# A new order of steps for a fused sigmoid-attention and token-mixing kernel

## The chip, the cores and the metric

The kernel runs on one core of one Trainium2 chip. The metric is the device time of one execution in microseconds (us). The engines named below are TensorE (PE), VectorE (DVE), ScalarE (ACT), GpSimd (POOL) and SyncE (SP), which issues most of the transfers between the chip's main memory and its on-chip memory (SBUF). TensorE writes its products to PSUM, a small memory of eight banks, from which DVE and ACT fetch ("evict") them.

## The reference

```python
# q, k, v: (8, 12, 448, 64) float32; w_q, w_k: (768, 64); w_out: (768, 768)
scores = q @ k^T / sqrt(64) - log(448)
attn   = 1 / (1 + exp(-scores)) @ v                      # per batch entry and head
x      = attn, heads side by side: (8, 448, 768)
wq, wk = x @ w_q, x @ w_k                                # (8, 448, 64)
W_tok  = wq @ wk^T / sqrt(64)                            # (8, 448, 448)
out    = relu(W_tok @ x) @ w_out                         # (8, 448, 768)
```

The kernel multiplies wk^T with x first (a 64 x 768 matrix, `tmp`) and then wq with that, so that the 448 x 448 matrix never exists.

## The kernel before

The work is cut into 24 quads: one batch entry u and four heads each, three quads to a batch entry. For every quad there are seven score steps (`scores`, letter S in the plan, 168 in all). A score step is four 64x64 matmuls (L319) into a pair of PSUM banks and one sigmoid on ACT over 128x896 (L324) into one of 16 buffers `at`. Seven value steps (`values`, letters P, p and R) multiply the sigmoids with v (L341). The last one evicts the sum to `xt`, either in one piece (L350) or in halves on DVE and ACT (L348).

Before its score steps a quad needs q and k as bf16 with the head dimension on the partitions. The letters of the plan choose the way for each quad:

- `a`, `b`: whole 128x128 transposes on PE (L237), one eviction for q and one for k (L293).
- `q`, `k`: 64x64 transposes on PE (L229), one eviction for both (L307).
- `c`, `d`: POOL exchanges blocks of 32-bit words between partition groups through a buffer named `swap`, in six copies of 32x448 words (`arrange`, L161, L164, L167); then DVE transposes q and k in blocks, with two instructions of 128x448 (L276).
- `r`, `s`, `z`: no exchange on POOL; DVE transposes whole (L269, two) and then in quarters (`quadrants`, L245, four of 32x448).

For `c` and `r` the casts to bf16 (L192) also reorder the data. v is cast at L209, the casts of `a` and `q` quads stand at L215. A cast goes to POOL unless the list of loads marks it with a dot or a capital, in which case a digit in the plan says when DVE (`1`) or ACT (`2`) does it.

For each batch entry the mixing part follows: `tr_x` (x and X) transposes `xt` back on PE (L379 small, L363 whole) with evictions at L392 and L368; `mlp_wqk` (W whole, L416; L tiled, L404, with an extra sum at L411 and L412) gives wq and wk; `mlp_wkn` (N) transposes wk (L431, evicted at L437); `mlp_tmp` (U, L445, or T, tiled, L460 with L464 and L465) and `mlp_mix` (M and G; L484, L498) follow, with the relu on DVE (L471) or ACT (L469). The output steps (O, Q, I) multiply with w_out: `out_pair` (L530) for the batch entries 2 to 5, `out_halves` (L570) and `out_chunk` (L611) for the others, evicted at L541, L543, L575, L576, L633 and L644, and stored.

Nothing is scheduled by a planner at build time. The string PLAN is the order: each letter issues one step, on whatever engines it uses, and every engine works in that order and waits where it must. The string BANKS names the PSUM banks of each step in turn. The string ORDER is the order of loads and casts; `pump_loads` issues a load as soon as the load eight places before it has been cast, and from the load number LATE on only two for each finished output. `pump` gives POOL its casts as soon as the buffers allow. An `F` is a filler matmul on zeros (L821). Before the plan starts, quad 0 is loaded, cast and transposed in parts (L676 to L803).

Of the kernel before, what the change touches and what calls it, by code (L numbers as in the profile page):

```python
# [17 lines left out]
def kernel(  # L18
# [12 lines left out]
    nc = tc.nc  # L31
# [4 lines left out]
    P = 128  # L36
# [11 lines left out]
    def pool(name, bufs, **kw):  # L48
# [16 lines left out]
    banks16 = banks.rearrange("p b x -> p (b x)").bitcast(BF16).rearrange("p (b x) -> p b x", b=8)  # L65

    BANKS = (
# [11 lines left out]
    )  # L79
    BANKS = BANKS.split()[::-1]  # L80

# [43 lines left out]
    def xt(u, j):  # L125
        return xts[u % 2 * NJ + j]


    TW = (1, 2,)


    PLAN = (
        "FFSSSFFKSSF11aSSbFFrSFSFSSFSqSPPsPPSPzkPSPSPPPSxSrSsPPPPSPPS"
        "PSPPPPSSXWzSSwWWSWWXSNSSPPPrSsPPUSPPzSPSPSPCMPPPSPSqkSSMSXSM"
        "SCcPPPSPPxSPdPSOSwwrSSwwWWxSOSSOsOSNPPSPPzCPSPPSIISISIcPSPdP"
        "PSPS2SPPOOSxSUSPPSMPPPcSPPSdOwWwSSMWWWoSMPPSPPPP1SSPcdOQSxSO"
        "OSSNCSOOXcdSSOOSTSPPPSrPPCPSPPCPPSPPPSPSOwowSSSwsOzOxSwwWPSP"
        "MSPPPPRSScSdXXOXoSMSOoNSMPPSPcPPSPPSUdSOSMOSOMoPSPPcPPSPSdPw"
        "WXWSMSWWWXSSONOScTSOSOSOOdSPOSrOSPPPGPPSPPPSPPsPSPOSPOSOzSQS"
        "XPcPPSPPPSPOSOdSOSxOlLlSLlLPSPPPxPP2GSPOOScOmdOSOOSNO1SQSTPP"  # L140
        "PcS1PPSPOPSOSOQSMOSOSOdScOOSdOMSOmOP2PSPPxSPPP12SOSOSOSxOllL"
        "SllcSLPPPSPPPSPOOdSxSOOSOSOSONQSTPSPPPSPPPSPPPxPPmPPLxLlMlGL"
        "lOOyOoNIItIiIMimIiMOoOOOoOoOOOOOOOOOoOO"
    )
    KIND = ["a"] + [t for t in PLAN if t in "qacer"]

    ld = {}
    SRC = dict(q=q, k=k, v=v)
# [3 lines left out]
    def arrange(n, eng):  # L152

        arranged.add(n)
        if KIND[n] in "er":
            return
        w = pq[n].rearrange("p e t i d y -> p e (t i d y)").bitcast(U32)
        z = p_one.tile([P, 2 * NI * 32], U32, tag="swap", name="swap")
        for g in range(2):
            lo, hi = slice(64 * g, 64 * g + 32), slice(64 * g + 32, 64 * g + 64)  # L160
            eng.tensor_copy(out=z[lo], in_=w[hi, 0])  # L161
        for g in range(2):
            lo, hi = slice(64 * g, 64 * g + 32), slice(64 * g + 32, 64 * g + 64)
            eng.tensor_copy(out=w[hi, 0], in_=w[lo, 1])  # L164
        for g in range(2):
            lo = slice(64 * g, 64 * g + 32)
            eng.tensor_copy(out=w[lo, 1], in_=z[lo])  # L167

    def load1(n, nm, eng):
        u, j = quads[n]  # L170
        if KIND[n] in "cer" and nm != "v":
            t = p_ld.tile([P, 2 * NI * HD], F32, tag="ld", name=nm + "32")
            eng.dma_start(
                out=t, in_=SRC[nm][u, 4 * j : 4 * j + 4].rearrange("h (p r) d -> (h p) (r d)", r=2 * NI),
            )
            ld[nm, n] = t
            return
        t = p_ld.tile([P, 2, NI * HD], F32, tag="ld", name=nm + "32")
        eng.dma_start(
            out=t,  # L180
            in_=SRC[nm][u, 4 * j : 4 * j + 4].rearrange(
                "(g h) (p i) d -> (h p) g (i d)", g=2, i=NI
            ),
        )
        ld[nm, n] = t

    def cast1(n, nm, e):
        if KIND[n] in "cer" and nm != "v":
            if n not in pq:
                pq[n] = p_c16.tile([P, 2, 2, NI, 32, 2], BF16, tag="qk16", name="qk16")  # L190
            f = pq[n]
            COPY[e](  # L192
                out=f[:, :, "qk".index(nm)].rearrange("p e i d y -> p e y i d"),
                in_=ld.pop((nm, n)).rearrange("p (y i e d) -> p e y i d", y=2, i=NI, e=2),
            )
            ld[nm + "16", n] = f
            if ("q16", n) in ld and ("k16", n) in ld:
                arrange(n, nc.gpsimd)
            return
        if nm == "v":  # L200
            t16 = p_v16.tile([P, 2, NI, HD], BF16, tag="v16", name="v16")
            if e == "d":
                u, j = quads[n]
                nc.gpsimd.dma_start(
                    out=t16.rearrange("p b i d -> p b (i d)"),
                    in_=v[u, 4 * j : 4 * j + 4].rearrange("(g h) (p i) d -> (h p) g (i d)", g=2, i=NI),
                )
            else:
                COPY[e](  # L209
                    out=t16.rearrange("p b i d -> p (b i d)"), in_=ld.pop((nm, n)).rearrange("p b x -> p (b x)"),  # L210
                )
            ld["v16", n] = t16
            return
        t16 = p_c16.tile([P, NI, 2, HD], BF16, tag=nm + "16", name=nm + "16")
        COPY[e](  # L215
            out=t16.rearrange("p i b d -> p b i d"),
            in_=ld.pop((nm, n)).rearrange("p b (i d) -> p b i d", i=NI),
        )
        ld[nm + "16", n] = t16
# [41 lines left out]
    def tr(n, nm, kind):  # L261
# [3 lines left out]
        if kind == "r":  # L265
# [2 lines left out]
            for e in range(2):  # L268
                nc.vector.transpose(out=qk[n][:, e].rearrange("p t i n -> p (t i n)").bitcast(F32), in_=w[:, e])  # L269
            return  # L270
        if kind in "cdef":
            assert n in arranged
            w = pq[n].rearrange("p e t i d y -> p e (t i d y)").bitcast(F32)[:, t]
            if t == 0:
# [417 lines left out]
    for t in wqks:  # L692
# [1 line left out]


    ORDER = (
# [4 lines left out]
    )  # L701
    BY = {"s": [], "v": []}
    for x in ORDER.split():
# [7 lines left out]
    done = dict.fromkeys("SPqkKxWNUMOCgz", 0)  # L711
    used, loaded, cast = set(), set(), set()

    LATE = 44
    ring = [("q", 0), ("k", 0)]

    allowed = [2]
# [94 lines left out]
    used |= {("q", 0), ("k", 0)}  # L812
    pump()

    ALIKE = dict(a="q", c="q", e="q", r="q", b="k", d="k", f="k", s="k", j="k", h="k", X="x", y="x", Y="x", g="g", z="z", L="W", l="W", T="U", t="U", I="O", i="O", Q="O", G="M", R="P")
    done["q"] = done["k"] = 1
    quads_r = []

    for t in PLAN:
# [18 lines left out]
        elif kind in "qk":  # L838
# [4 lines left out]
            tr(c, kind, t)  # L843
            if t in "df":
                used.add(("q", c))
            if t not in "cers":
                used.add((kind, c))
                pump()
        elif t == "g":
# [69 lines left out]
```

## Time and profile before

| | |
|---|---|
| median of 3 timed runs | 183.79 us (182.34 to 184.23) |
| the profiled execution, first to last instruction | 180.4 us; the page gives no other time for it |
| PE busy | 170.3 us (94%) |
| ACT busy | 159.0 us (88%) |
| DVE busy | 143.7 us (80%) |
| POOL busy | 122.9 us (68%) |
| granted TensorE clock | 1.000 |
| moved by DMA | 47.29 MB, mean 262 GB/s |

The page counts an engine as busy from the start of an instruction to its end; overlapping instructions are counted once, so a group's busy time can be below its count times its mean. Idle time of an engine is put down to what released it. A busy PE is not PE at its peak, since matmuls are pipelined and their ends are modelled.

### The profile page before, as it was taken

What the parts mean: (1) busy time and instruction counts of PE and PEld (TensorE: products, weight loads), DVE (VectorE), ACT (ScalarE), POOL (GpSimd) and SP (SyncE); (2) the same over time, 40 slices, a digit from 0 to 9 for tenths busy, and PEclk for the clock granted to TensorE, in tenths of its full rate; (3) what the DMA queues carried; (4) which work ended last, traced back from release to release, by engine and by line L of the source; (5) the groups of instructions that cost most, each with busy time, mean ns of one, the idle gap of its engine ahead of it and who ended that gap; (6) DMA issues with size and microseconds to landing.
All of it is one profiled execution on the core that took longest, in us unless ns stands there. A gap on an engine that the chain in (4) does not pass through costs nothing.

```text
span 180.4 us, 7849 instructions
## 1 busy us (share of the span) xinstructions
PE 170.3 (94%) x3412; PEld 114.1 (63%) x3412; DVE 143.7 (80%) x226; ACT 159.0 (88%) x208; POOL 122.9 (68%) x167
## 2 busy tenths in 40 slices
PE   7898899889999999999999999999999999999990
PEld 7444445444675555546667786677888888888660
DVE  3566899998988896989999999978789885868351
ACT  4599999999999999999999999998999989976310
POOL 1076899798999999999999999889978810010000
PEclk9999999999999999999999999999999999999999
DMA  5999999999999989699997999968596432505876
GB/s 169 353 394 346 325 385 376 283 304 366 339 305 358 349 266 299 226 318 349 279 318 277 257 307 329 372 215 272 137 336 166 131 88 48 137 4 123 207 196 174
DMA packets 24914, 47.29 MB, mean 262 GB/s; under 512 B 3888, under 2 KB 18480, under 8 KB 24880
## 3 DMA queue, kind: packets, MB, share of 16 engines
q1 hardware_dynamic: 23600, 44.64, 76.8%
q0 software_dynamic: 800, 1.18, 3.6%
q10 hardware_dynamic: 480, 0.98, 1.5%
q8 instruction: 26, 0.43, 0.9%
q14 instruction: 8, 0.07, 0.1%
HBM read 35.78 MB, written 11.01 MB: 259 GB/s over the span
## 4 chain that ended last, share of the span: by engine, by line
PE 61%; DMA 16%; ACT 7%; POOL 5%; DVE 4%; SPq 3%; issue 2%; POOLq 0%
PE banks L530 15%; PE banks L341 11%; PE banks L319 11%; PE banks L611 9%; DMA k<-in_k_dram 8%; ACT at L324 7%; DMA v<-in_v_dram 5%; DMA w<-in_moe_w_k_dram 4%; PE banks L570 3%; POOL qk L192 2%; PE banks L404 2%; PE banks L416 2%; PE banks L379 2%; PE banks L363 2%; PE banks L484 1%
## 5 line engine op out<-in xcount | busy, mean ns | idle before, releaser
L324 ACT ACTIVATE at<-banks 128x896 bf16<-128x896 f32 x168 | 139.8, 951 | 2.9 <-PE banks L319 2.4
L319 PE MATMUL banks<-qk 64*64 64x448 bf16 x672 | 62.0, 357 | 3.3 <-ACT at L324 2.0
L341 PE MATMUL banks<-at,v 64*64 64x448 bf16 x672 | 47.3, 351 | 0.8 <-ACT at L324 0.7
L319 PEld LDWEIGHTS <-qk 64*64 64x64 bf16 x672 | 25.7, 105 | 21.5 <-issue 13.3
L530 PE MATMUL banks<-wout,mx 64*64 64x384 bf16 x672 | 36.2, 323 | 0.0
L192 POOL CAST qk<-k 128x896 bf16<-128x896 f32 x19 | 22.7, 1196 | 10.1 <-DMA k<-in_k_dram 9.7
L341 PEld LDWEIGHTS <-v 64*64 64x64 bf16 x672 | 23.2, 106 | 8.4 <-issue 1.8
L350 DVE CAST xt<-banks 128x896 bf16<-128x896 f32 x22 | 23.8, 1084 | 2.5 <-PE banks L341 2.0
L530 PEld LDWEIGHTS <-mx 64*64 64x64 bf16 x672 | 22.6, 107 | 4.5 <-issue 0.2
L611 PE MATMUL banks<-wout,mx 128*128 128x384 bf16 (+1 forms) x138 | 24.4, 320 | 0.0
L192 POOL CAST qk<-q 128x896 bf16<-128x896 f32 x18 | 21.5, 1193 | 2.5 <-DVE qk L276 1.0
L471 DVE TENSOR_SCALAR mx<-banks 128x1024 bf16<-128x1024 f32 (+3 forms) x22 | 21.3, 970 | 1.9 <-PE banks L484 0.7
L209 POOL CAST v<-v 128x896 bf16<-128x896 f32 x22 | 20.6, 952 | 1.8 <-DMA v<-in_v_dram 1.3
L611 PEld LDWEIGHTS <-mx 128*128 128x128 bf16 x138 | 12.3, 98 | 9.8 <-issue 3.2
L167 POOL COPY qk<-swap 32x448 uint32<-32x448 uint32 x28 | 16.3, 584 | 1.6
L276 DVE STREAM_TRANSPOSE qk<-qk 128x448 f32<-128x448 f32 x28 | 17.0, 628 | 0.5 <-POOL qk L164 0.4
L161 POOL COPY swap<-qk 32x448 uint32<-32x448 uint32 x28 | 15.6, 556 | 2.5 <-DVE qk L192 0.8
L164 POOL COPY qk<-qk 32x448 uint32<-32x448 uint32 x28 | 15.6, 555 | 1.6
L245 DVE STREAM_TRANSPOSE qk<-qk 32x448 f32<-32x448 f32 x24 | 15.3, 636 | 0.6
L413 POOL COPY wq<-wqk 64x448 bf16<-64x448 bf16 x3 | 1.7, 556 | 15.8 <-DVE wqk L412 15.8
L644 DVE COPY o<-banks 128x384 f32<-128x384 f32 x12 | 6.6, 553 | 5.7 <-PE banks L611 5.3
L392 DVE COPY xn<-banks 128x1024 bf16<-128x1024 bf16 (+1 forms) x14 | 8.8, 625 | 2.8 <-PE banks L379 2.7
(89 smaller groups left out, 203.8 us busy)
## 6 DMA issues: line engine op xcount, KB each, us to landing
q<-in_q_dram SPq DMA_DIRECT2D x24, 448.0 KB, 6.3
v<-in_v_dram SPq DMA_DIRECT2D x24, 448.0 KB, 6.0
k<-in_k_dram SPq DMA_DIRECT2D x23, 448.0 KB, 6.9
out_dram<-o SPq DMA_DIRECT2D x50, 192.0 KB, 4.2
wout<-in_moe_w_out_dram POOLq DMA_DIRECT2D x2, 576.0 KB, 11.6
wout<-wout SPq DMA_DIRECT2D x12, 96.0 KB, 6.4
out_dram<-o ACTq DMA_DIRECT2D x4, 192.0 KB, 3.2
k<-in_k_dram SPq DMA_DIRECT2D x1, 256.0 KB, 4.8
```

Of the source, the lines that this page charges most:

```text
L161: eng.tensor_copy(out=z[lo], in_=w[hi, 0])
L167: eng.tensor_copy(out=w[lo, 1], in_=z[lo])
L192: COPY[e](out=f[:, :, "qk".index(nm)].rearrange("p e i d y -> p e y i d"), in_=ld.pop((nm, n)).rearrange("p (y i e d) -> p e y i d", y=2, ...
L209: COPY[e](out=t16.rearrange("p b i d -> p (b i d)"), in_=ld.pop((nm, n)).rearrange("p b x -> p (b x)"),)
L276: nc.vector.transpose(out=qk[n][:, t].rearrange("p t i n -> p (t i n)").bitcast(F32), in_=w)
L319: nc.tensor.matmul(sc[HALF[h], g, 0:S], qk[n][HALF[g], h, 1, i, :], qk[n][HALF[g], h, 0].rearrange("p i n -> p (i n)"), start=True, stop=True,
L324: inst = nc.scalar.activation(at, sc[:, :, 0:S], ACTF.Sigmoid, bias=attn_bias, scale=attn_scale)
L341: nc.tensor.matmul(ps[HALF[g], h, 0:S], ld["v16", n][HALF[h], g, i, :], ats[n, i][HALF[h], g, :], start=(i == 0), stop=(i == NI - 1),)
L350: read(fb, COPY[eng](out=xt(u, j)[:, :, 0:S], in_=ps[:, :, 0:S]))
L471: inst = nc.vector.tensor_scalar(dst, ps, moe_scale, 0.0, ALU.mult, ALU.max)
L530: nc.tensor.matmul(ps[HALF[x], y, 0:NB], mx[HALF[y], u, b, 64 * (i - 3 * y) : 64 * (i - 3 * y) + 64], wout16[HALF[y], slot(y, b), x * NB : ...
L611: nc.tensor.matmul(ps, mxs[w][:, 2 * S * c + m * P : 2 * S * c + (m + 1) * P], wout16[:, c, w0:w1], start=(c == 0), stop=(c == NC - 1),)
```

## The change

PLAN, BANKS and ORDER are replaced by new strings, and LATE falls from 44 to 30. The quads' ways change: before, one `a`, two `q`, six `r` and fourteen `c` follow quad 0; after, four `q`, sixteen `c` and three of a new kind `v`. For a `v` quad the six exchange copies of `arrange` are issued on DVE, just ahead of its two block transposes, in place of POOL. The way with transposes in quarters is no longer used.

Counted over the whole program, the order of the instructions shows further: 13 v casts on DVE instead of 1 (POOL 11 instead of 22, ACT none instead of 1); five `xt` evictions in halves instead of two; 21 small `tr_x` instead of 14 and 3 whole instead of 10; four tiled `mlp_wqk` instead of three; three tiled `mlp_tmp` instead of five; five filler matmuls instead of ten. The output steps keep their forms and numbers; 48 of the L530 matmuls that stood after the last score step stand before it.

```diff
-    KIND = ["a"] + [t for t in PLAN if t in "qacer"]
+    KIND = ["a"] + [t for t in PLAN if t in "qacerv"]
...
     def arrange(n, eng):
 
         arranged.add(n)
-        if KIND[n] in "er":
+        if KIND[n] in "r":
             return
...
-        if KIND[n] in "cer" and nm != "v":
+        if KIND[n] in "crv" and nm != "v":
...
             if ("q16", n) in ld and ("k16", n) in ld:
-                arrange(n, nc.gpsimd)
+                if KIND[n] == "v":
+                    arranged.add(n)
+                else:
+                    arrange(n, nc.gpsimd)
...
-        if kind in "cdef":
+        if kind == "v":
+            arrange(n, nc.vector)
+        if kind in "cdefv":
...
     ORDER = (
-        ".q1 .k1 k2 q2 q3 v0 w2 k3 v1 k4 q4 v2 w0 k5 q5 w1 v3 W5 v4 q6 k6 w4 k7 v5 q7 v6 q8 k8 k9 "
-        "q9 v7 q10 v8 k10 v9 k11 q11 k12 k13 v10 .q12 q13 v11 v12 v13 q14 k14 k15 q15 v14 q16 k16 "
-        "v15 q17 k17 k18 q18 q19 v16 v17 v18 k19 V19 W3 q20 .q22 q21 k20 W6 k21 .k22 v20 q23 k23 "
-        "v21 .v22 v23 "
+        "q1 .k1 v0 .k2 q3 .q2 v1 k3 q4 k4 w0 k5 .v2 q5 w1 v4 .v3 q6 k6 w4 k7 v5 q7 .k8 q8 k9 q9 "
+        "v6 v7 q10 v8 q11 k10 .k11 q12 k12 .v9 v11 .v10 k13 q13 .k14 .v12 v13 q14 q15 k15 v14 "
+        "q16 .k16 .v15 k17 q17 .v16 k18 .q19 q18 .v17 k19 k20 .v18 q20 .v19 q21 k21 k22 .v20 q22 "
+        ".v22 q23 k23 v21 .v23 "
     )
...
-    LATE = 44
+    LATE = 30
```

The beginning and the end of the plan, before and after:

```diff
-        "FFSSSFFKSSF11aSSbFFrSFSFSSFSqSPPsPPSPzkPSPSPPPSxSrSsPPPPSPPS"
+        "FFSSSFFKSSFSq1SkSRSP1Sp1SSpPqkRPSpSPSpSvppRPSSXdS1SqSkSRpPSS"
...
-        "SllcSLPPPSPPPSPOOdSxSOOSOSOSONQSTPSPPPSPPPSPPPxPPmPPLxLlMlGL"
-        "lOOyOoNIItIiIMimIiMOoOOOoOoOOOOOOOOOoOO"
+        "OQSoNcSQSOSQdoSOSOSRR1ppSppRSTQSQSo1SORPSPPPPpRpSpRGRMPRRmlll"
+        "ylllyIiyNIIIUiiGmiMQOQoOOOooOOoOoQoOOQQ"
```

More of the change, by code (lines that the diff above doesn't have):

```diff
@@ L126, in xt @@
         return xts[u % 2 * NJ + j]
-    TW = (1, 2,)
+    TW = (1, 2, )
     PLAN = (
-        "FFSSSFFKSSF11aSSbFFrSFSFSSFSqSPPsPPSPzkPSPSPPPSxSrSsPPPPSPPS"
[L134 to L141, printed above, removed]
-        "SllcSLPPPSPPPSPOOdSxSOOSOSOSONQSTPSPPPSPPPSPPPxPPmPPLxLlMlGL"
-        "lOOyOoNIItIiIMimIiMOoOOOoOoOOOOOOOOOoOO"
+        "FFSSSFFKSSFSq1SkSRSP1Sp1SSpPqkRPSpSPSpSvppRPSSXdS1SqSkSRpPSS"
+        "pSPRPWWXSW1xSWWSWRSPRSNpRcpPSSdUqSkSxSSMRppSpMSRSRPSRSMPSRPp"
+        "SxPPSSW1WSXSWWcSSWdWOSvSNOQSOCdSQSSUQSvSRPPRPSRPPpRdSRRRSPSo"
+        "OGSSMoOSppPSSPPP1PcSdWWOWCSMSWWQWSxi1SISicSINSoSOPCdSpRCxSp1"
+        "CCpPSSPoOSpRScxPdRPSpPSUSppSRSRRR11SPOOSxcdSQoSMSOOSPRPSxpPG"
+        "RPSScWWWWWWSxSQdSxOSNMRpRSpRSRPocSoSxQSdOSUSpPSPpppS1PQS1OSM"
+        "OSOcllSdlllRlmPRPpSPPSOQS1GONQSxocdSOSTSQQSxpPSpPRS1o1RSPoSO"
+        "PScdOSRPPGpRSPSQ1oSxoScOdSLLLSLLLPSpRRGpPSP1QSoSxQGOSSocOSxQ"
+        "SdOPPSPPRSNRRSToSoSocdSO1QSoSMoSQRpGPRxSPpRGLLLLcSSLLoQSdOxS"
+        "OQSoNcSQSOSQdoSOSOSRR1ppSppRSTQSQSo1SORPSPPPpRpSpRGRMPRRmlll"
+        "ylllyIiyNIIIUiiGmiMQOQoOOOooOOoOoQoOOQQ"
     )
-    KIND = ["a"] + [t for t in PLAN if t in "qacer"]
+    KIND = ["a"] + [t for t in PLAN if t in "qacerv"]
     ld = {}
@@ L187, in cast1 @@
     def cast1(n, nm, e):
-        if KIND[n] in "cer" and nm != "v":
+        if KIND[n] in "crv" and nm != "v":
             if n not in pq:
@@ L813 @@
     pump()
-    ALIKE = dict(a="q", c="q", e="q", r="q", b="k", d="k", f="k", s="k", j="k", h="k", X="x", y="x", Y="x", g="g", z="z", L="W", l="W", T="U", t="U", I="O", i="O", Q="O", G="M", R="P")
+    ALIKE = dict(v="q", a="q", c="q", e="q", r="q", b="k", d="k", f="k", s="k", j="k", h="k", X="x", y="x", Y="x", g="g", z="z", L="W", l="W", T="U", t="U", I="O", i="O", Q="O", G="M", R="P")
     done["q"] = done["k"] = 1
@@ L845 @@
                 used.add(("q", c))
-            if t not in "cers":
+            if t not in "cersv":
                 used.add((kind, c))
```

22 rows, old and new, of the table BANKS are left out of this document.

## The prediction

> **What bounds the kernel now.** I read the span first, then busy time by stretch, then the groups of ScalarE (ACT) and VectorE (DVE), then the order of time at both ends. Line numbers are those of the kernel before.
>
> ```profile
> span 180.4 us, 7849 instructions
> ```
>
> The page gives this execution no other time; the three timed runs (182.34 to 184.23, median 183.79) lie 1.9 to 3.8 us above its span. I work on the span and add the difference to 183.79.
>
> ```profile
> core 0: us, PE busy (x) PEld busy (x) DVE busy (x) ACT busy (x) POOL busy (x), PEclk, DMA share, GB/s
> ...
> 6.97:46.90 39.93, 35.83 (x673) 18.16 (x666) 33.82 (x50) 39.93 (x50) 31.85 (x37) 1.00 1.06 352
> 46.90:150.30 103.40, 102.64 (x2177) 71.48 (x2178) 90.38 (x132) 100.55 (x127) 89.76 (x124) 1.00 0.84 268
> 150.30:156.50 6.20, 6.20 (x178) 5.26 (x174) 4.07 (x7) 6.20 (x10) 0.00 (x0) 1.00 0.53 130
> 156.50:180.40 23.90, 19.66 (x356) 14.43 (x348) 12.36 (x25) 9.79 (x21) 0.56 (x1) 1.00 0.52 134
> ```
>
> I cut the span where the first sigmoid starts (6.97), the 50th (46.9), the 162nd (150.3), and where the last ends (156.5). Each row gives the length and then the busy time of each engine. Between first and last sigmoid ACT is almost never idle: this stretch is as long as ACT's work. The last stretch has no sigmoid and runs at the pace of TensorE (PE). DVE is busy 90.4 of the 103.4 us in the middle, so it has 13.0 us in hand there.
>
> ```profile
> 6.97 54.62 ACT L324 ACTIVATE at<-banks 128x896 bf16<-128x896 f32 x67 [0.99 <-PE banks L319]
> ```
> ```profile
> L324 ACT ACTIVATE at<-banks 128x896 bf16<-128x896 f32 x168 | 139.8, 951 | 2.9 <-PE banks L319 2.4
> L644 ACT COPY o<-banks 128x384 f32<-128x384 f32 x9 | 4.4, 489 | 7.1 <-PE banks L611 6.5 <-ACT mx L469 0.4 <-ACT at L324 0.2
> L469 ACT ACTIVATE mx<-banks 128x448 bf16<-128x448 f32 x6 | 3.2, 564 | 0.2 <-PE banks L498 0.2
> L469 ACT ACTIVATE mx<-banks 128x1024 bf16<-128x1024 f32 x2 | 2.0, 1017 | 0.0
> L541 ACT COPY o<-banks 128x384 f32<-128x384 f32 x4 | 1.9, 481 | 0.0
> ...
> L543 ACT COPY o<-banks 128x768 f32<-128x768 f32 x2 | 1.6, 800 | 0.6 <-PE banks L530 0.6
> L469 ACT ACTIVATE mx<-banks 128x512 bf16<-128x512 f32 x2 | 1.2, 600 | 0.5 <-PE banks L484 0.5
> L348 ACT CAST xt<-banks 128x448 bf16<-128x448 f32 x2 | 1.1, 560 | 0.0
> L209 ACT CAST v<-v 128x896 bf16<-128x896 f32 x1 | 0.9, 930 | 0.0
> L411 ACT COPY wpart<-banks 128x448 f32<-128x448 f32 x1 | 0.6, 571 | 0.0
> ```
>
> The first 67 sigmoids follow each other every 54.62/67 = 0.815 us, though one lasts 0.951: each overlaps the next by 0.136. All waiting before sigmoids is 2.9 us; no plan can win more than that from ACT's gaps.
>
> **The change, part by part.**
>
> *ACT before the last sigmoid.* The sigmoids stay 168. Beside them stood 5 L644, 1 L348, 1 L543, 2 relus of 512, 2 of 1024, 4 L541 and 1 v cast: 9.9 us by these rows. After there are 3 L644, 4 L348, 7 relus of 512, 1 of 1024, 1 of 448, 1 L411 and 3 L541: 11.5 us. That is 1.6 more in four more instructions, each overlapping by 0.136: **+1.1 us** on the path that sets the end.
>
> *The start.* Quad 1 changes from whole transposes with an eviction each to small transposes with one eviction of both.
>
> ```profile
> 11.28 0.62 DVE L293 COPY qk<-banks 128x896 bf16<-128x896 bf16 x1 [0.76 <-PE banks L237]
> ```
> ```profile
> L307 DVE COPY qk<-banks 128x1792 bf16<-128x1792 bf16 x2 | 2.2, 1086 | 1.3 <-PE banks L229 1.3
> ```
>
> The eighth score step waits for the second of them, which ends at 11.28 + 0.62 = 11.9; with 1.09 it ends at 12.4, and the step's own matmuls and two hand-overs bring it past 12.7, where the eighth sigmoid is due (6.97 + 7 x 0.815). I take **+0.3 us** (0 to 1.0, the upper end if the six exchanges of quad 3 on DVE also come late). Five fewer filler matmuls cost nothing: PE waits there.
>
> *DVE in the middle stretch.* I count in the order of the instructions the DVE steps between the 50th sigmoid and the last transposes of quad 23, before and after.
>
> ```profile
> L276 DVE STREAM_TRANSPOSE qk<-qk 128x448 f32<-128x448 f32 x28 | 17.0, 628 | 0.5 <-POOL qk L164 0.4
> L245 DVE STREAM_TRANSPOSE qk<-qk 32x448 f32<-32x448 f32 x24 | 15.3, 636 | 0.6
> L471 DVE TENSOR_SCALAR mx<-banks 128x1024 bf16<-128x1024 f32 x8 | 9.7, 1219 | 1.0 <-PE banks L484 0.7
> L543 DVE COPY o<-banks 128x768 f32<-128x768 f32 x8 | 7.6, 956 | 1.2 <-issue 0.4 <-PE banks L530 0.4 <-ACT at L324 0.2
> ...
> L644 DVE COPY o<-banks 128x384 f32<-128x384 f32 x12 | 6.6, 553 | 5.7 <-PE banks L611 5.3 <-issue 0.3
> ...
> L471 DVE TENSOR_SCALAR mx<-banks 128x512 bf16<-128x512 f32 x2 | 1.4, 686 | 0.0
> L192 DVE CAST qk<-q 128x896 bf16<-128x896 f32 x2 | 1.3, 674 | 0.0
> L209 DVE CAST v<-v 128x896 bf16<-128x896 f32 x1 | 1.1, 1060 | 0.0
> ...
> L215 DVE CAST k<-k 128x896 bf16<-128x896 f32 x1 | 0.6, 627 | 0.0
> ```
>
> - The 12 quarter transposes go: -12 x 0.636 = -7.6. Full transposes rise from 30 to 33: +1.9.
> - Outputs: +3 x 0.956 and +2 x 0.553 = +4.0. Relus: -4 x 1.219 + 5 x 0.686 = -1.4. One more L192: +0.7. All other evictions together about -1.7.
> - v casts rise from 1 to 9. One on DVE took 1.06, while a cast of the same size took 0.63 at the start, before POOL had work: +8 x 0.63 to 1.06 = +5.0 to 8.5. I take 0.75, **+6.0**.
> - Word exchanges: 12 here (two of the three groups). No DVE row shows one. Half of the 0.63 cast (half as many words) gives 0.31 below; the 0.636 of the 32x448 transpose is the upper bound: +3.7 to 7.7. I take 0.45, nearer the copies, **+5.4**.
>
> Sum: +7.3 (4.6 to 12.1), so DVE needs 97.7 us (95.0 to 102.5). ACT's own length of the stretch becomes 103.4 + 0.6 = 104.0, the 0.6 being ACT's extra work that falls in it. DVE keeps 6 us in hand where it had 13. Its best stretch shows how full it can run:
>
> ```profile
> 20.00:40.00 20.00, 17.95 (x354) 9.89 (x350) 19.06 (x27) 20.00 (x26) 17.81 (x24) 1.00 1.08 338
> ```
>
> At 19.06 of 20 the 97.7 us take 102.5, and nothing slips. At the middle stretch's own 90.38/103.40, the same waits again, they take 111.8: 7.8 late. What is late next is an eviction that frees a PSUM bank pair, or a transpose; queued behind it on DVE stands the rest, PE's next score step waits for it, and ACT for PE. In the order before, the last step that makes a quad's q and k stands on average 3.4 sigmoids ahead of the first score step that uses it; after, 2.6, and for quads 7, 16 and 20 none at all. I take **+3.0 us**, between 0 and 7.8.
>
> ```profile
> 127.67 0.67 DVE L192 CAST qk<-q 128x896 bf16<-128x896 f32 x1
> 127.79 1.57 POOL L167 COPY qk<-swap 32x448 uint32<-32x448 uint32 x2
> ```
> ```profile
> 141.90 2.20 POOL L209 CAST v<-v 128x896 bf16<-128x896 f32 x2
> 142.25 1.06 DVE L209 CAST v<-v 128x896 bf16<-128x896 f32 x1
> ```
>
> Where such a DVE cast meets POOL, one of them stretches: the pair of POOL copies took 1.57, and the v cast that came 0.35 us into a POOL cast took 1.06. [...]
>
> *POOL* loses 7 of its v casts there and gets two more exchanges of its own; with 89.8 of 103.4 busy it stays below ACT. *Loads* are reordered and held back earlier (30 instead of 44), but each stands at least 7 sigmoids, 5.7 us, ahead of its cast, and casts have a quad's time in hand: nothing, or 1 us if a landing falls late. *PE's* new forms (small transposes for whole ones, tiled products for whole ones) nearly cancel.
>
> *The tail.*
>
> ```profile
> 158.94 0.97 PE banks L530 x24
> ```
>
> After the last score step stood 48 output matmuls of L530, two runs of 24 at 0.97: 1.9 us. They now stand before it, so the tail shrinks by up to 1.9. They also covered the waits for xn and wqk there; the other fillers (96 matmuls of L570) stay. Ahead of it they meet a PE that shows 102.64 of 103.40 us busy; that it takes them without delay is the open end. I take **-1.5 us** (-1.9 to 0).
>
> Sum: 1.1 + 0.3 + 3.0 - 1.5 = **+2.9**: span 183.3, time **186.7 us**.
>
> **The rivals.**
>
> 1. *The tail decides, faster.* Place: the end, 48 matmuls earlier. Price: -1.9, and half of ACT's 2.9 us of waiting, -1.5, against +1.1: 181.5. It decides if DVE keeps its last transposes ahead of the score steps. For it: 19.06 of 20 shows that DVE can. Against: the lead ahead of the score steps shrinks by a quarter.
> 2. *No slip, no more won.* 1.1 + 0.3 - 1.5: 183.7. For it: DVE's waits are waits for PE, which shrink when DVE falls behind.
> [...]
>
> That the change doesn't do what it says is excluded by the order of its instructions: no quarter transposes, 18 exchanges on DVE, output matmuls of L530, L570 and L611 as before.
>
> **How the numbers follow.** Forecast 0.42, rival 1 0.23, rival 2 0.22, rival 3 0.13. A measurement of this kernel tells about 1% from no change (181.95 to 185.63). Slower: 0.42 + 0.13 = 0.55; within: 0.22; faster: 0.23. The range reaches to rival 1 below and to rival 3 above: 181.5 to 191.7. The forecast's own range is 184 to 189.
>
> **What would show it.** Right: DVE over 96% busy between the 50th and the 162nd sigmoid, that stretch 105 us or longer, waits of L319 on DVE that before doesn't have, a tail of 22 to 23 us. Wrong: exchanges near 0.3 us, v casts near 0.63, DVE still with 8 us in hand, the last sigmoid ending before 157.6.

## The result, and the profile after

| | before | after |
|---|---|---|
| median | 183.06 us (181.49 to 184.23) | 195.19 us (194.87 to 197.42) |
| after / before | | 1.078, 95% interval 1.067 to 1.090 |
| profiled execution | span 180.4 us | span 192.8 us |

The change costs 12.1 us by the medians (6.6%); the ratio, taken against the runs of before made beside it, says 7.8%, some 14 us. The prediction said +2.9 us, and its range ended at 191.7 us. An execution over 1.5% above the fastest of its kernel counts as slow, and the times and ratios below leave the slow ones out; only the traces of experiments 2 and 4 and of the first two kernels of experiment 6 are of slow executions. Line numbers of the kernel after are five or so higher than those of before: L329 is the sigmoid, L324 its matmuls, L346 the values, L355 the `xt` eviction, L281 the block transposes, L212 the v casts.

The first view gives busy time by stretch of the kernel after, cut where the prediction cut (to 0.3 us): first sigmoid, 50th, 162nd, end of the last. Columns: from:to, length, busy time of PE, PE's weight loads, DVE, ACT and POOL with their counts, granted clock, DMA.

```profile
span 192.8 us, 8387 instructions
```
```profile
6.10:51.21 45.11, 35.38 (x770) 19.11 (x764) 32.83 (x44) 40.47 (x50) 29.35 (x37) 0.96 1.01 334
51.21:163.48 112.27, 106.29 (x2397) 71.82 (x2396) 98.37 (x148) 103.12 (x132) 90.19 (x123) 0.98 0.77 243
163.48:170.10 6.62, 6.62 (x154) 5.47 (x147) 4.51 (x8) 6.62 (x11) 0.00 (x0) 1.00 0.43 101
170.10:192.80 22.70, 18.18 (x326) 12.24 (x317) 10.64 (x23) 9.25 (x20) 0.55 (x1) 0.97 0.50 135
```

Against before, the first stretch is 5.2 us longer, the middle 8.9, the third 0.4, the tail (the stretch behind the last sigmoid) 1.2 shorter, and the first sigmoid comes 0.9 earlier: +12.4, the difference of the spans. The loss is easier to see with the cut at the 65th sigmoid; the first two rows are of before, the next two of after.

```profile
6.97:59.11 52.14, 48.00 (x912) 26.50 (x908) 44.45 (x68) 52.14 (x65) 43.15 (x54) 1.00 1.05 346
59.11:156.50 97.39, 96.67 (x2112) 68.39 (x2104) 83.81 (x120) 94.54 (x122) 78.46 (x107) 1.00 0.79 252
```
```profile
6.10:69.21 63.11, 50.68 (x944) 26.29 (x941) 49.61 (x70) 54.18 (x67) 39.77 (x48) 0.95 0.92 299
69.21:170.10 100.89, 97.61 (x2376) 70.10 (x2366) 86.10 (x129) 96.03 (x124) 79.78 (x111) 1.00 0.76 239
```

Before, ACT is busy in every moment of its first 64 sigmoids (52.14 of 52.14). After, it stands idle for 8.9 us there (63.11 - 54.18), and the clock of PE was not granted in full. So 11.0 us are lost in the first third and 3.5 in the rest. What PE and ACT waited for:

```profile
ACT at L329 <- PE banks L324: 11.6, 14, 2.4
...
PE banks L324 <- DVE xt L355: 2.7, 1, 2.7
...
PE banks L324 <- DVE wkn L442: 2.5, 1, 2.5
...
PE banks L384 <- issue: 2.2, 2, 1.7
```

Each row: who waited, for what, us in all, times, longest. Before, the longest wait of a score step on DVE was 0.5 us. The two of 2.7 and 2.5 us stand right behind an exchange on DVE. DVE's own timeline at the first (start, duration, engine, line):

```profile
16.48 1.08 DVE L355 CAST xt<-banks 128x896 bf16<-128x896 f32 x1
17.59 1.42 DVE L161 COPY swap<-qk 32x448 uint32<-32x448 uint32 x2
19.04 1.45 DVE L164 COPY qk<-qk 32x448 uint32<-32x448 uint32 x2
20.52 1.27 DVE L167 COPY qk<-swap 32x448 uint32<-32x448 uint32 x2
21.82 0.65 DVE L281 STREAM_TRANSPOSE qk<-qk 128x448 f32<-128x448 f32 x1
22.39 1.05 DVE L355 CAST xt<-banks 128x896 bf16<-128x896 f32 x1
```
```profile
23.50 0.38 PE L324 MATMUL banks<-qk 64*64 64x448 bf16 x4 [2.68 <-DVE xt L355]
```
```profile
23.93 2.54 ACT L329 ACTIVATE at<-banks 128x896 bf16<-128x896 f32 x3 [1.92 <-PE banks L324]
```

The six copies of quad 3 hold DVE from 17.59 to 21.8. The `xt` eviction behind them ends at 23.44; PE's score step needs its bank and starts at 23.50; the sigmoid follows at 23.93, 1.92 us late. At quad 8 (50.7 to 56.0) the same happens ahead of the `wkn` eviction. And PE's clock halves behind the wait (the eighth column of numbers is the granted clock):

```profile
24.20:24.30 0.10, 0.10 (x4) 0.07 (x7) 0.10 (x1) 0.10 (x1) 0.10 (x1) 0.50 1.19 430
...
27.60:27.70 0.10, 0.10 (x8) 0.06 (x4) 0.00 (x0) 0.10 (x1) 0.10 (x1) 1.00 0.87 323
```

It falls at 24.15, is 0.50 for some 3.4 us and 1.00 again at 27.6; and once more it is halved from 58.3 to 61.7, behind the second wait.

### The profile page after: what moved, and what is told of

Its sections match the earlier page's. It is cut to its first block, busy times and chain, and to the rows that moved or that the text cites. A ratio compares the mean times of both kernels' runs of the same rounds, so it can differ in the third digit from the quotient of the medians.

```text
span 192.8 us, 8387 instructions
## 1 busy us (share of the span) xinstructions
PE 171.3 (89%) x3678; PEld 112.6 (58%) x3679; DVE 148.9 (77%) x235; ACT 161.9 (84%) x212; POOL 120.8 (63%) x165
## 4 chain that ended last, share of the span: by engine, by line
PE 73%; DVE 13%; DMA 5%; issue 3%; ACT 2%; SPq 2%; DVEq 0%
PE banks L346 16%; PE banks L324 14%; PE banks L535 14%; PE banks L616 11%; DMA q<-in_q_dram 5%; PE banks L575 3%; PE banks L384 3%; PE banks L409 2%; PE banks L450 2%; ACT at L329 2%; DVE swap L161 2%; DVE qk L164 2%; PE banks L421 2%; DVE xt L355 2%; DVE qk L281 2%
## 5 line engine op out<-in xcount | busy, mean ns | idle before, releaser
L329 ACT ACTIVATE at<-banks 128x896 bf16<-128x896 f32 x168 | 141.4, 932 | 12.5 <-PE banks L324 11.6
L324 PE MATMUL banks<-qk 64*64 64x448 bf16 x672 | 63.7, 363 | 8.7 <-DVE xt L355 2.7
L346 PE MATMUL banks<-at,v 64*64 64x448 bf16 x672 | 48.1, 358 | 2.3 <-issue 1.2
L324 PEld LDWEIGHTS <-qk 64*64 64x64 bf16 x672 | 26.3, 107 | 26.8 <-issue 17.9
L346 PEld LDWEIGHTS <-v 64*64 64x64 bf16 x672 | 23.1, 109 | 11.9 <-issue 5.1
L355 DVE CAST xt<-banks 128x896 bf16<-128x896 f32 x19 | 20.5, 1081 | 6.1 <-PE banks L346 5.9
L281 DVE STREAM_TRANSPOSE qk<-qk 128x448 f32<-128x448 f32 x38 | 23.3, 628 | 0.1
L192 POOL CAST qk<-k 128x896 bf16<-128x896 f32 x15 | 17.9, 1193 | 8.1 <-DVE qk L281 7.4
L164 POOL COPY qk<-qk 32x448 uint32<-32x448 uint32 x32 | 19.6, 613 | 1.9
L476 DVE TENSOR_SCALAR mx<-banks 128x448 bf16<-128x448 f32 (+3 forms) x23 | 19.2, 844 | 1.6 <-PE banks L503 1.3
L397 DVE COPY xn<-banks 128x1024 bf16<-128x1024 bf16 (+1 forms) x21 | 13.7, 652 | 4.5 <-PE banks L384 4.4
L548 DVE COPY o<-banks 128x768 f32<-128x768 f32 x11 | 10.5, 957 | 2.9 <-ACT at L329 2.9
L212 POOL CAST v<-v 128x896 bf16<-128x896 f32 x11 | 10.7, 980 | 2.9 <-DMA v<-in_v_dram 2.6
L384 PEld LDWEIGHTS <-xt 64*64 64x64 bf16 x672 | 9.8, 108 | 4.7 <-issue 3.4
L384 PE MATMUL banks<-ident,xt 64*64 64x64 bf16 x672 | 10.0, 193 | 2.3 <-issue 2.2
```

The costliest lines, as they stand in the source:

```text
L192: COPY[e](out=f[:, :, "qk".index(nm)].rearrange("p e i d y -> p e y i d"), in_=ld.pop((nm, n)).rearrange("p (y i e d) -> p e y i d", y=2, ...
L281: nc.vector.transpose(out=qk[n][:, t].rearrange("p t i n -> p (t i n)").bitcast(F32), in_=w)
L324: nc.tensor.matmul(sc[HALF[h], g, 0:S], qk[n][HALF[g], h, 1, i, :], qk[n][HALF[g], h, 0].rearrange("p i n -> p (i n)"), start=True, stop=True,
L329: inst = nc.scalar.activation(at, sc[:, :, 0:S], ACTF.Sigmoid, bias=attn_bias, scale=attn_scale)
L346: nc.tensor.matmul(ps[HALF[g], h, 0:S], ld["v16", n][HALF[h], g, i, :], ats[n, i][HALF[h], g, :], start=(i == 0), stop=(i == NI - 1),)
L355: read(fb, COPY[eng](out=xt(u, j)[:, :, 0:S], in_=ps[:, :, 0:S]))
```

## Why an exchange copy takes up to 1.27 us

The groups of DVE after:

```profile
L161 DVE COPY swap<-qk 32x448 uint32<-32x448 uint32 x6 | 4.9, 812 | 0.2
L164 DVE COPY qk<-qk 32x448 uint32<-32x448 uint32 x6 | 4.2, 699 | 0.2
L167 DVE COPY qk<-swap 32x448 uint32<-32x448 uint32 x6 | 3.0, 503 | 0.2
L212 DVE CAST v<-v 128x896 bf16<-128x896 f32 x13 | 10.4, 799 | 0.0
```

The prediction took 0.45 us for a copy, with 0.31 and 0.64 as bounds. The means are 0.81, 0.70 and 0.50. Single copies beside POOL's instruction at that time show why:

```profile
17.62 1.15 POOL L218 CAST q<-q 128x896 bf16<-128x896 f32 x1
18.00 1.01 DVE L161 COPY swap<-qk 32x448 uint32<-32x448 uint32 x1
...
51.18 1.38 POOL L192 CAST qk<-q 128x896 bf16<-128x896 f32 x1
51.55 1.27 DVE L161 COPY swap<-qk 32x448 uint32<-32x448 uint32 x1
...
60.92 0.38 DVE L164 COPY qk<-qk 32x448 uint32<-32x448 uint32 x1
```

POOL's cast ends at 18.77 and DVE's copy at 19.01; POOL's at 52.56 and DVE's at 52.82. A copy that came into a running POOL instruction ends some 0.24 us behind it (0.24 and 0.26 by these rounded rows), though the one still had 0.77 us to go and the other 1.01. Where POOL was idle (60.92), a copy takes 0.38. Beside a busy POOL the two engines go one instruction each in turn (at quad 8 four copies of 0.82 to 1.27 us, each ending behind one of four POOL casts of 1.08 to 1.38), and a burst of six runs at POOL's pace: 4.2 us for quad 3, 5.3 for quad 8, 3.1 for quad 9, where six alone would take 2.5. The 18 copies take 12.1 us in all, 5.2 more than alone. The block transposes are not held up (shortest, median and longest in ns):

```profile
L281 DVE STREAM_TRANSPOSE qk<-qk x38: 601/634/645, 21.8 to 160.5; 128x448 f32<-128x448 f32 x38
```

So beside POOL such a copy takes the rest of POOL's instruction and 0.24 us more; these rows show the size of the wait, and not by what way the one engine holds up the other.

## The experiments

Theory A: the exchange stands in DVE's queue ahead of evictions, and PE and its clock pay for it. Rivals: B, the new order itself; C, the v casts on DVE; later D, pauses of PE in small transposes; E and F, that PE has no slack or has it; G, that each copy costs its wait for POOL and not its width. Ratios are to the runs of before made beside each, with 95% intervals.

**1. The exchange back on POOL.**

```diff
-  PLAN "... pSvppRP ... WOSvSNO ... SUQSvSRP ..."
+  PLAN "... pScppRP ... WOScSNO ... SUQScSRP ..."
```

> The changed kernel with the 18 exchange copies of quads 3, 8 and 9 on POOL instead of DVE (letters v become c), all else as it is. Theory A (the burst of six copies in DVE's queue keeps evictions and so PE's score steps waiting, and PE's clock drops behind the wait; about 10 of the 13.5 us between first and last sigmoid are lost before the 61st sigmoid): at least 6 us come back, 189 us or less, and the slices at 24-28 and 58-62 us show a granted clock of 1.00. Theory B (the new order of steps itself leaves too short leads, and PE stalls in its small transposes): under 2 us come back, 193 us or more. POOL has 3 x 3.4 us more to do in the first 60 us, so a later cast may take 1 to 2 us of the gain back.

193.86 us, 1.062 (1.051 to 1.072). Theory A's number was missed. The two waits on DVE went, and others came in their place:

```profile
35.04 0.41 PE L232 MATMUL banks<-ident,q 64*64 64x64 bf16 x28 [2.17 <-POOL q L218]
...
57.97 1.14 PE L346 MATMUL banks<-at,v 64*64 64x448 bf16 x20 [2.34 <-POOL v L212]
```

POOL's casts of quad 4 and of a v stand behind the exchange in POOL's queue now. In this order POOL has no room for the exchange either. The half-clock windows did not go but came elsewhere (from 12.1 and 36.0 us; the mean granted clock from 6.5 to 66.0 us is 0.94).

**2. The v casts on POOL, where DVE had them.**

```diff
-        cast_now(nm, n, e)
+        cast_now(nm, n, "g" if nm == "v" else e)
```

> The changed kernel with the 13 v casts that stand on DVE issued on POOL at the same places of the order; DVE keeps the 18 exchange copies. It takes 13 x 0.80 = 10.4 us of work from DVE. Theory A (the exchange bursts): under 2 us come back, 193 us or more. Theory C (the v casts, which last 0.80 us on average instead of 0.62 and collide with POOL's work, make DVE late): 4 us or more come back, 191 us or less. POOL gets 13 casts of about 1.2 us, so that a slowdown would mean that POOL has become late.

222.07 us, 1.217 (1.195 to 1.239): POOL is late, and by far. This says nothing on theory C.

```profile
PE banks L346 <- POOL v L212: 22.3, 6, 6.0
```

**3. Before, with three exchanges on DVE.** The letters c of quads 7, 9 and 10 become v, with the lines for v added.

> The kernel before with one thing of the change: the six exchange copies of its quads 7, 9 and 10 are issued on DVE, just ahead of the block transposes, instead of on POOL. Theory A (bursts in DVE's queue): the three bursts of 2.4 to 5 us keep evictions waiting, 3 to 8 us slower, 186 to 191 us. Theory B (order and leads): within 1%, 181.5 to 185.5. The prediction's price (18 x 0.45 us on a DVE with 13 us in hand): 0 to 1 us slower.

193.89 us, 1.063 (1.053 to 1.073): some 11.5 us for this one part (10.6 in the texts below, by the medians of all runs), more than theory A said and against the prediction's 0 to 1. Three waits of PE make it, behind which ACT stands idle for 3.9, 2.2 and 4.8 us:

```profile
PE banks L503 <- DVE xt L355: 3.6, 1, 3.6
PE banks L616 <- DVE xn L397: 3.4, 1, 3.4
PE banks L384 <- DVE xt L355: 2.5, 1, 2.5
```
```profile
68.31 0.80 DVE L161 COPY swap<-qk 32x448 uint32<-32x448 uint32 x2 [1.41 <-POOL qk L167]
69.14 0.80 DVE L164 COPY qk<-qk 32x448 uint32<-32x448 uint32 x2
69.97 0.80 DVE L167 COPY qk<-swap 32x448 uint32<-32x448 uint32 x2
...
71.36 1.05 DVE L355 CAST xt<-banks 128x896 bf16<-128x896 f32 x1
```

Here POOL is idle and a copy takes its 0.38, and 2.5 us ahead of an eviction are still too much; besides, DVE first waits 1.41 us for POOL to be done with the one `swap` buffer. Only 3 of the 18 copies met a POOL instruction (all 18 take 8.5 us, 1.6 more than at 0.38 each), so waits for POOL are not needed for such a loss: the place in DVE's queue does most of it. The 13 us that DVE had in hand over 103 us are some forty short waits, the longest of 1.1 us; none could hold a burst.

**4. The exchange behind the evictions that PE waited for.**

```diff
-  "SvppRPSSXd" ... "SvSNOQSOCd"
+  "SppRPvSSXd" ... "SSNOQSOCvd"
```

> The changed kernel with the exchange of quad 3 issued one eviction (xt) later and that of quad 8 three evictions (wkn and two o) later in DVE's queue, so that the evictions for which PE waited 2.68 and 2.53 us no longer stand behind it; the amount of work on DVE is the same. If the place in the queue costs the time (theory A): the two waits go, the granted clock at 24-28 us and in the slice of quad 8 stays near 1.00, and 2 to 5 us come back (190 to 193 us). If the amount of work on DVE or its collisions with POOL cost it: under 1 us comes back, as the delay only moves to the block transposes and the score steps behind them.

194.84 us, 1.068 (1.058 to 1.079): no gain that can be told. Moving the burst moves the wait: in this trace PE's score steps wait 3.7 us for an `xn` eviction and 2.3 for an `xt`.

**5. Each exchange in three pairs, with evictions between.** Two more letters issue the first and the second pair, v the third:

```diff
-  "SpSvppRPSSXdS1S" ... "XSWWcSSWdWO" ... "SSUQSvSRPP"
+  "SpS3ppRPS4SXvdS1S" ... "XSWWcS3SWd4WO" ... "SSUQ3S4SvRPP"
```

> The changed kernel with each exchange on DVE issued in three pairs of copies at three places of the plan, with evictions between them (an xt and an xn eviction for quad 3, a wqk eviction for quad 8; for quad 9 the pairs stay together but come two score steps earlier), same amount of work. If the burst is what keeps evictions waiting: the waits of 2.68 and 2.53 us fall below 1.5, no half-clock window follows, and 3 to 6 us come back, 189 to 192. If the amount of DVE work at that place counts: under 1 us, 194 to 196.

197.37 us, 1.083 (1.072 to 1.094): no gain either. The first wait fell to 1.1 us and the second went, but PE waited 1.8 us for a `wqk` eviction that now stood behind a pair and 1.2 for an `xt`, and two half-clock windows came as before (mean granted clock of the span 0.982). So it is not only the burst as one piece.

**6. Copies of 8 words, whole transposes, short v casts.** The next four runs shorten the work.

```diff
-            eng.tensor_copy(out=z[lo], in_=w[hi, 0])
+            eng.tensor_copy(out=z[lo, :e], in_=w[hi, 0, :e])   # e = 8 on DVE; the other copies alike
```

> The changed kernel with the 18 exchange copies on DVE cut from 448 to 8 words wide, in the same places of every queue (the exchange of quads 3, 8 and 9 is left out but for these few words). What it gains is the whole price of the exchange on DVE, with no other engine loaded for it. Theory A (the bursts cost the time): 6 to 10 us come back, 185 to 189 us. Theory B (the order itself, with its pauses of PE): 2 to 4 us come back, 191 to 193 us, about what the exchange took of ACT's waits before the 61st sigmoid (8.9 us there, of which 4.3 stand right behind a DVE exchange).

190.17 us, 1.041 (1.031 to 1.050): 3.7 of the 7.8 points come back, between the theories in us and near theory A by the ratio.

> The changed kernel with all tr_x steps of plan letter x in whole 128x128 transposes (8 for 32, evicted as before with one instruction of the same size); all else as it is. Theory D (PE's instruction supply: PE pauses with no releaser in the profile, 1.72, 0.90 and 0.46 us long, in or right behind runs of small transposes, which take 64 instructions in 0.45 us): the pauses go and 2 to 4 us come back, 191 to 193 us. If the pauses are only where PE would wait anyway: under 1 us.

194.51 us, 1.068 (1.058 to 1.077): the pauses went but for one of 0.71 us, and nothing came back that can be told. Theory D's sum lacked a term: a whole step is dearer on PE (21 whole steps with 168 matmuls take 13.0 us; 21 small ones with 672, before the edit, 10.0). So what the pauses cost by themselves stays open.

```profile
L368 PE MATMUL banks<-ident,xt 128*128 128x128 bf16 x168 | 13.0, 221 | 0.4 <-ACT at L329 0.4
```


> The changed kernel with both edits: the exchange copies on DVE cut to 8 words (the exchange is left out but for these) and whole transposes for small ones. Theories A and D together: 9 us or more come back, 186 us or less. If the order of steps has other short leads that come up as soon as these go: 188 us or more, less gain than the sum of the two edits alone.

190.01 us, 1.043 (1.033 to 1.053).

> The same two edits, and besides the 13 v casts of DVE cut from 896 to 64 columns into a spare tile, while the value steps of these quads read the v that POOL cast last (so these v are left out). DVE is relieved of about 18 us of work in all, below what it does in the kernel before. Theory C (the v casts on DVE make its evictions late): 2 to 4 us below the kernel with two edits. Theory B (the leads of the new order do not depend on DVE's load): under 1 us below it, and what is then left above 183 us is the order's.

190.57 us, 1.045 (1.036 to 1.054). The last two edits add nothing that can be told to the short copies alone, as theory B said. But narrow copies are not free, as the rows of the last run show:

```profile
47.92 1.19 POOL L195 CAST qk<-q 128x896 bf16<-128x896 f32 x1
48.06 1.07 DVE L164 COPY swap<-qk 32x8 uint32<-32x8 uint32 x1
...
49.90 0.94 POOL L220 CAST v<-v 128x896 bf16<-128x896 f32 x1
50.01 0.85 DVE L167 COPY qk<-qk 32x8 uint32<-32x8 uint32 x1
...
56.04 0.16 DVE L167 COPY qk<-qk 32x8 uint32<-32x8 uint32 x1
```

A copy of 8 words takes 0.16 us alone and 1.07 behind POOL; it ends 0.02 us after POOL does. Six of them at quad 8 lasted 4.1 us, where full ones last 5.3. Beside a busy POOL the width is the small part of a burst's length.

**7. No copies, then no v casts either.**

```diff
-        if kind == "v":
-            arrange(n, nc.vector)
```

> The changed kernel without the 18 exchange copies on DVE at all (the exchange of quads 3, 8 and 9 is left out; their transposes stay). In the run with copies of 8 words, 12 of the 18 still met a running POOL instruction and lasted 0.59 us on average, ending 0.02 us behind it, where those that met none lasted 0.16. Theory G (what costs is that each copy waits out POOL's instruction, six times in a row, not its width): the three bursts go altogether, 187 to 189.5 us, 2 us or more below the run with short copies. Theory B (the order itself keeps the rest): as that run, 190 to 193.

187.86 us, 1.038 (1.029 to 1.046). This lies in theory G's range, but the 2 us below the run with short copies go with faster runs of before beside it (181.17 against 182.92): the ratios, 1.038 and 1.041, cannot be told apart. Only the traces point theory G's way. The first 64 sigmoids take 54.15 us here (rows further down) and 56.97 with short copies and whole transposes:

```profile
6.30:63.27 56.97, 49.24 (x872) 26.07 (x869) 44.55 (x70) 54.04 (x67) 38.78 (x48) 1.00 0.99 324
63.27:165.37 102.10, 102.10 (x2016) 69.80 (x2006) 86.85 (x129) 96.51 (x124) 79.39 (x111) 1.00 0.76 239
```

Now the v casts go too:

```diff
+            if e == "v":
+                ld.pop((nm, n)); ld["v16", n] = last16[0]; return
```

> The same, and also without the 13 v casts on DVE (the value steps of these quads read the v that POOL cast last, so their v are left out). These casts met POOL's work as well and lasted 0.80 us on average, 0.62 where they came first or alone. If their waits keep evictions back like the exchange's: 2 to 4 us below the run without the exchange. If they stand where DVE has time: under 1 us below it. What then remains above 183 us is the price of the new order of steps itself.

185.54 us, 1.024 (1.017 to 1.031), 2.3 us below the run beside it, and none of the runs of the two overlap: the gain is inside theory C's range. The first two rows are without copies, the next two without the casts too, cut at the 65th sigmoid:

```profile
6.99:61.14 54.15, 46.80 (x945) 25.60 (x941) 37.14 (x52) 53.23 (x66) 38.51 (x48) 1.00 1.02 335
61.14:164.88 103.74, 98.28 (x2376) 70.39 (x2369) 87.20 (x129) 96.18 (x124) 79.45 (x111) 1.00 0.75 237
```
```profile
6.87:60.71 53.84, 47.21 (x945) 25.39 (x941) 35.58 (x49) 53.11 (x67) 38.26 (x48) 1.00 1.02 338
60.71:159.97 99.26, 97.54 (x2376) 70.63 (x2366) 79.17 (x118) 95.78 (x124) 76.13 (x111) 1.00 0.79 247
```

Without the copies the first 64 sigmoids take 54.15 us instead of 63.11, with the clock at 1.00; but the rest takes 103.74 instead of 100.89, so a third of that gain is lost again behind it. Without the casts the rest takes 99.26. That the casts kept evictions back there is not shown: pauses of PE that no instruction ended take 3.4 us of the 103.74 (0.56, 1.81 and 1.04; the longest below), and none of the 99.26 (one of 1.04 there is put down to ACT).

```profile
115.75 0.34 PE L382 MATMUL banks<-ident,xt 64*64 64x64 bf16 x18 [1.81 <-issue]
```

By the ratios, of the 7.8% that the change costs about 4.0 are the exchange on DVE (1.078 to 1.038), 1.4 go with the v casts on DVE (1.038 to 1.024), and 2.4 remain; each ratio is known to about one point. By the spans of the profiled runs (192.8, 187.4, 182.6, and 180.4 before) it would be 5.4, 4.8 and 2.2 us, but there the run without copies is the slowest of its three. Shown is that the exchange on DVE costs 5 to 7 us here; the rest is split less surely.

**8. The clock.** Fillers ahead of the stalled instructions keep PE busy and change nothing else:

```diff
-  "... S1S ..."
+  "... S1FFFFFFFFFFS ..."     # ahead of the 20th and the 55th score step, bank 0 and bank 2
```

> The changed kernel with 10 filler matmuls of 128x512 zeros (about 2.1 us) put on PE ahead of each of the two score steps that waited 2.68 and 2.53 us for an eviction behind a DVE exchange; the fillers go into a bank that nobody needs then, and nothing else changes. If the half-clock windows (3.41 us each, from 24.15 and 58.28 us) come from PE standing idle and cost time of their own: the two windows go, and the two gaps of ACT behind them (1.04 and 1.3 us) with them, 1.5 to 3 us faster than the changed kernel, 192 to 193.5. If the clock only drops where PE has time anyway: within 0.7 us of it, 194.5 to 196.

193.78 us, 1.066 (1.055 to 1.076); the mean granted clock of the span rose from 0.979 to 0.997. The step is in the direction expected, but the intervals overlap.

> The kernel before with the full exchange of quads 7, 9 and 10 on DVE, and 12, 8 and 12 filler matmuls (2.5, 1.7 and 2.5 us) ahead of the three PE instructions that waited 3.42, 2.52 and 3.60 us behind it. If the two half-clock windows of that run (from 45.1 and 72.4 us) cost time of their own: they go, and of its 10.6 us 2 to 4 come back, 190 to 192. If not: within 1 us of it, 193 to 195.

190.70 us, 1.049 (1.041 to 1.058), against 1.063 (1.053 to 1.073) without fillers: some 3 us, with the clock from 0.982 to 0.995, though ACT still waits 3.1, 2.2 and 3.6 us at the three places. The intervals overlap by a little, so that the half clock costs time of its own is likely and not shown.

> The kernel before with the exchange of quads 7, 9 and 10 on DVE as in the run that was 10.6 us slower, but 8 words wide instead of 448 (the exchange of these three quads is left out but for these words). If the length of the six copies is the cause: back to within 2 us of the kernel before, 182 to 185. If the place of the wait is (DVE now waits for these quads' casts in its queue, and POOL's later casts for DVE): 187 or more.

187.73 us, 1.032 (1.025 to 1.040). Copies of 8 words, at places where POOL mostly rests, halve the price: 3.2 of 6.3% are left, so that length and place each have about half. A PE wait of 2.3 us is among what is left, and DVE ahead of it waited for the `swap` buffer:

```profile
63.34 0.36 DVE L162 COPY swap<-qk 32x8 uint32<-32x8 uint32 x2 [1.42 <-POOL qk L168]
```

**9. How much slack PE has.** Four runs change PE's work alone:

```diff
+        if i == 3 and 6 <= n <= 21:          # before: four more matmuls of zeros onto the open sum
...
-        for b in range(3 * part, 3 * part + 3):
+        for b in (3 * part, 3 * part + 2):   # after, and before: a third of out_pair left out
```

> The kernel before with 16 more value steps of zeros (four 64x64 matmuls of 448 columns each, added onto the open sum of quads 6 to 21, so that the output does not change). A value step takes 0.277 us of PE by the kernel before (29.9 us for 108 steps), so this is 4.4 us of PE work. Theory E (PE, 99% busy behind the first 60 sigmoids, has no slack: what is added to it or lost by it there comes out at the end in full): 3.5 to 4.5 us slower, 186.5 to 188. Theory F (ACT sets the pace and a busy PE has slack behind its modelled ends): under 1.5 us slower.

184.68 us, 1.011 (1.002 to 1.020): 2 us for 4.4 us of work, between the theories.

> The changed kernel with the middle third of each out_pair part left out (224 of its 672 matmuls, so that the outputs of batch entries 2 to 5 lack a third of their terms): 12.2 us of PE work less (36.6 us for 672), all of it between the 64th sigmoid and the last. Theory E: 6 us or more faster than the changed kernel (189 or less), until ACT sets the pace; the waits and half-clock windows before the 61st sigmoid stay as they are, so that it does not come down to 183. Theory F, or waits on DVE as the whole cause: under 2 us faster.

192.84 us, 1.056 (1.045 to 1.067): 2.4 us by the medians and 2.2 points by the ratio, for 12 us less PE work. That is between the theories, and far from 12: the changed kernel waits, and PE's load is not what bounds it.

> The same third left out of the kernel before (208 of its matmuls before the last sigmoid, 11.3 us of PE). By its ACT, which waits 2.9 us in all before sigmoids, it can gain 3 us at most: 1 to 3 us faster, 180 to 182. If it gains 6 us or more, the kernel before was bound by PE alone and ACT's row was misread.

179.48 us, 0.985 (0.976 to 0.994): some 3 us, about what ACT's waits allow.

> The kernel before with the last 48 matmuls of L530 (four O steps, 1.9 us of PE) moved from behind the last score step to between the last three, through the bank pair 01; 01 and 67 change names behind that. The prediction took 1.5 us off the tail for this move. Theory F: 1 to 1.9 us faster, the last sigmoid where it was. Theory E: the last sigmoid ends 1 to 1.9 us later and the tail is that much shorter, the time within 0.7 us of before.

186.55 us, 1.021 (1.011 to 1.030): slower by 3.8 us, which neither theory had. Its last two stretches, from the 65th sigmoid to the end of the last, and the tail:

```profile
59.20:159.66 100.46, 98.91 (x2141) 71.49 (x2137) 84.00 (x119) 95.34 (x122) 77.14 (x106) 1.00 0.77 240
159.66:183.40 23.74, 18.57 (x343) 13.27 (x331) 12.61 (x25) 9.05 (x20) 0.56 (x1) 1.00 0.51 134
```

The 48 matmuls lengthen the stretch ahead by 3.1 us, and the tail stays at 23.7: waits that they had covered come up in their place, one of 1.0 us of L431 on the `wqk` sum among them.

## Why the prediction was wrong, point by point

- *The direction* was right, and so were the ways to see it: waits of score steps on DVE, a middle stretch over 105 us (112.3), a tail of 22 to 23 us (22.7). DVE over 96% busy did not come (88%), and one of the signs against the forecast did: DVE had 13.9 us in hand in the middle stretch, more than the 8 that were to refute the forecast, and the time was lost all the same.
- *DVE's sum* came out and did not matter. The prediction put DVE's need at 97.7 us; it is 98.37. In part this is luck: the 12 exchange copies took 8.0 us and not 5.4, and other work came out lower by nearly as much. The step that failed is the next one, which turned the sum into time by the mean load of the stretch ("at 19.06 of 20 ... nothing slips"). DVE is busy 98.37 of 112.27 us, 88% and not over 96: it has more time in hand than the sum left it, and PE waits for it, for 2.5 us in one piece behind the burst of quad 8. The term was **+3.0 us (0 to 7.8); the stretch grew by 8.9, of which 0.6 were given to ACT's own work, so 8.3 stand against it**.
- *The start* was the other term that was mis-sized: +0.3 (0 to 1.0), and the first stretch measured +5.2. Quad 1's eviction costs what was said (the ninth sigmoid starts 6.7 us behind the first, 6.4 before). Quad 3's exchange, which the prediction let end at "1.0 if it comes late", costs the 1.92 us of the chain above and 1.1 more in the half-clock window behind it; a third wait of ACT there, 1.2 us, follows the PE pause of 1.7 us that no instruction ended.
- *The price of an exchange copy*, 0.45 (0.31 to 0.64), is right for a resting POOL (0.38) and wrong for a working one (up to 1.27). The upper bound was taken from the transposes, which POOL did not hold up (0.60 to 0.65 us for a block of 128x448). The rows of the kernel before that showed a cast at 1.06 beside POOL were quoted, and went into the price of the v casts alone.
- *The v casts* at 0.75 measured 0.74 in the stretch (0.80 over the whole program). All 13 together go with 1.4% of the time, by a way that is not shown.
- *ACT*, +1.1: its other work was 11.5 us as worked out. Between first and last sigmoid ACT is busy 150.2 us instead of 146.7; that is 3.5 more, of which 1.6 are this work. Nearly all the rest is in the sigmoids themselves, busy for 141.4 us instead of 139.8: 14 of them waited for PE instead of 6, and one that waits does not overlap the one ahead.
- *The tail*, -1.5: measured -1.2. The reason given for it is not shown, since the same move by itself gave nothing to the tail of the kernel before.
- *POOL, "nothing"*: it stayed below ACT, but two runs show that its order has no room: 3 exchanges more made PE wait 2.2 and 2.3 us, and 13 casts cost some 25 (1.217 against 1.078).
- *PE's clock* was in no term. It was 1.00 all through the trace of before, where PE's longest pause between the first sigmoid and the last is 0.6 us.
- *The rivals*: 1 and 2 needed DVE on time. Rival 3's chance of 0.13 and the upper end of the range, 191.7, rest on every copy on DVE waiting out POOL's instruction. No run shows that: of the 18 exchange copies 11 came into one here, which lengthened the bursts, and in experiment 3, which lost as much, 3 did. Even so that end lies 3.5 us below the measured time.

Open: what makes the last 2.4%, steps of the new order or the pauses of PE told of below (3.1 us between the first sigmoid and the last, 0.6 before), which no run took away by themselves; by what way the v casts cost time; and what the exchange would cost in a form that POOL does not hold up, as it did not hold up the block transposes, which was not tried.

## What to carry to other kernels

Idle time of an engine that is added up over a stretch is not slack at a place: before putting work into an engine's queue, look at what stands behind it there and how long its consumer can wait (here an `xt` eviction stood behind 4.2 us of copies, and PE waited 2.7). Price a VectorE copy like these by the GpSimd instruction that it will meet (up to 1.27 us here), and not by itself alone (0.38). To test such a price, take the instruction away, since a narrow one can still wait (up to 1.07 us here for 0.16 of its own).

## What the hardware showed that was not expected

- A VectorE exchange copy of 32x448 words that came into a running GpSimd instruction ended 0.24 to 0.27 us after it, each of the 11 in the kernel after; of 32x8 words it ended 0.02 us after it (12 of the 18 in the run with copies of 8 words). Alone they take 0.38 and 0.16. Block transposes of 128x448 took 0.60 to 0.65 in the kernel after, the 30 that overlapped GpSimd's work as well as the 8 that did not.
- PE's clock in the kernel after was halved for 3.41 us from 24.15 and from 58.28, behind waits of 2.68 and 2.53 us, and from 191.40 to the end, when PE had no work left. In the first case it began 0.65 us after PE had work again, in the second 1.42. The third experiment had two such stretches (from 45.1 and 72.4 us) for three waits of 3.42, 2.52 and 3.60 us, and none behind the second. In the trace of after, the stretches of one clock (1.00 for 20.48 us, 0.50 for 3.41, 1.00 for 30.72, 0.50 for 3.41, 1.00 for 129.71) are all whole multiples of 3.413. Cut into pieces of that length at the changes, PE was busy for 0.73, 1.24 and 0.29 us of the 3.41 just ahead of the three halvings; behind every other piece the clock stayed at 1.00, and the least busy of those had 1.87.
- PE paused with no releaser for 1.72, 0.90 and 0.46 us between the first sigmoid and the last of the kernel after, and for 0.63 in the kernel before, three times of the four in a run of small transposes; without the copies (experiment 7) it was 0.62, 0.56, 1.81 and 1.04, at other places in part. Three of the four pauses of before and after end 1.2 to 1.5 us after a transfer of 16 KB has landed on the queue that the pages list as `q8 instruction` (28 transfers in the kernel after), the one of 0.46 ends 0.8 after. So PE may have waited for instructions there; no run tests it.
